# A third buffer for spectra and turned units, spectra asked for three slots ahead, and a later input turn, in a long-convolution and maxout kernel

## Chip, cores and metric

One Trainium2 chip, one of its cores. The metric is the device time of one execution in microseconds (us), the median of several runs. TensorE (PE) does the matrix products, VectorE (DVE), ScalarE (ACT) and GpSimd (POOL) the elementwise work; SyncE (SP) only issues DMAs here. Weight loads of TensorE stand in the profile as PEld. An engine's queue of instructions that it issues without computing has a "q" behind its name (SPq).

## What is computed

Four sequences (batches) of 12,544 positions with 128 channels go through a long convolution with a gate, and then through a feed-forward block with a maximum of three products:

```python
h_filt = (np.maximum(pos_emb @ w1, 0.0) @ w2) * window      # one filter per channel
u = x * v
y = irfft(rfft(u, n=2*S) * rfft(h_filt, n=2*S))[:, :S, :]   # along the positions
x = (x * y).reshape(B * S, D)
h = np.maximum(np.maximum(x @ w1, x @ w2), x @ w3)          # D = 128, DFF = 768
out = h @ w_out
```

All data are float32. The filter is so short in effect that the kernel needs only part of it; `lin` and the differences of weights let it do one of the three products of the feed-forward as a correction.

## The kernel before

**The convolution of one batch.** The Fourier transform is split into two stages of matrix products. The input of a batch comes in 32 units `u` (four channels each). A unit goes through these steps:

- `u_load` (L330): two DMAs on SP bring x and v of the unit into tiles `ut` of the pool `inq`, which has two buffers for each of the two (L856).
- `u_mul` (L342): DVE multiplies them in place.
- `u_planes` (L361): POOL clears the padding (L364) and splits the numbers into 16-bit halves (L365), into a tile `planes` of tag `x` (four buffers, `state["xb"]`).
- `u_dma` (L369): a transposing DMA on SP turns them, into `turned` of tag `xs` (five buffers, `state["xsb"]`).
- `u_join` (L375): ACT and DVE each put one half together again in a tile `uT` of the pool `utp` (two buffers; two units share a tile).
- `u_first` (L386): TensorE does the first stage, ACT or DVE copies the result into `spec`, which holds the whole batch.

Then follow 45 pairs `g` of frequencies. `w_load` (L393) brings the tables `wt` of the second stage (a = 0) and of the inverse stage (a = 1) from DRAM; they share tags and buffers with the `ut` tiles. `h_load` (L399) brings the filter's spectrum `ht` of the pair with two DMAs of SP; its tile has the tag `uT` of the pool `utp`, so spectra and turned units take turns in the same two buffers. `g_second` is the matrix product, `g_butterfly` (DVE) and `g_swap` (ACT) prepare the complex product, `g_re` (L430) and `g_im` (L433) multiply by the two halves of `ht` on DVE, `g_sum` (L436) adds on POOL, `g_unfold` (L442, tile `ab`) on DVE prepares the inverse, `g_third` is TensorE's inverse product, `g_pair` (L468) and `g_store` finish and send the result to DRAM (`zd`).

**The feed-forward.** Sixteen pairs of blocks of each batch, 12 steps (slots) each. `t_load` (L521) brings `zt` and the gate `xT` for a block with two and four DMAs on SP, `t_last` does the last stage of the inverse transform (TensorE, tile `yps`) and the gate (DVE, L558 and L560). In each slot `up` (L565) makes one hidden tile: two products `pa` and `pb` (TensorE), Relu of the first (ACT, L570), the maximum with the second (DVE, L573). POOL forms sums of hidden tiles (L589), and `products` (L608) makes the output products (L619), which are stored from ACT's queue. Hidden tiles named h11 have four buffers (`BUFS`, L584), as the others.

**What sets the order.** The schedule is written by hand: the program's order on each engine is the order in which the calls below are made. The prologue (up to L849) transforms the filter, runs the whole convolution of batch 0, and takes in the first six units of batch 1; in it `utp` holds turned units too. After that the main loop (L890) goes through the feed-forward of batch b and spreads the convolution of batch b + 1 over its 192 slots. `conv_steps` (L475) gives each step of the convolution a slot by a formula; steps of one slot run in the order in which `at` was called, those marked "late" last. For 32 units the distance of pairs `per_pair` is 165/64.2 = 2.57 slots and that of units 0.6 of it, 1.54; for batch 1, with 26 units left, 2.72 and 1.63. In a slot the loads for the feed-forward (`bring`) come first, in slots 0 and 1 of a pair of blocks, then `up`, the output products and sums, `t_last` in slots 5 and 8, and then the convolution's steps.

Every engine takes its instructions in the program's order. A DMA of SP that needs a buffer not yet free waits in SP's queue, and the DMAs behind it in the queue wait with it.

Of the kernel before, what the change touches and what calls it, by code (L numbers as in the profile page):

```python
# [70 lines left out]
def kernel(  # L71
# [147 lines left out]

    utp = ctx.enter_context(tc.tile_pool(name="utp", bufs=2))
    pro = ExitStack()
    pin = pro.enter_context(tc.tile_pool(name="pin", bufs=1))
    lwp = pro.enter_context(tc.tile_pool(name="lwp", bufs=3))
    eye = pin.tile([P, P], FP32, name="eye")
    w_sb[0] = pin.tile([D, DFF], FP32, name="w_sb0")
    inp = pro.enter_context(tc.tile_pool(name="inp", bufs=3))
    fin = ExitStack()
    inp0 = fin.enter_context(tc.tile_pool(name="inp0", bufs=3))  # L230
    sml = fin.enter_context(tc.tile_pool(name="sml", bufs=1))
# [243 lines left out]
    def conv_steps(b, done):  # L475


        out = []

        def at(slot, late, fn, *args):  # L480
            out.append((slot, late, len(out), fn, args))

        per_pair = 165 / (NK + 0.6 * (NU - done))
        for u in range(done, NU):
            s = (u - done) * 0.6 * per_pair + 12
            at(max(0, int(s) - 13), 0, u_load, b, u)
            at(int(s) - 8, 0, u_mul, u)
            at(int(s) - 7, 0, u_planes, u)  # L490
            at(int(s) - 6, 0, u_dma, u)
            at(int(s), 0, u_join, u)
            for h in range(2):
                at(int(s + 2 + 0.3 * per_pair * h), 1, u_first, u, h)
        s0 = int((NU - done) * 0.6 * per_pair) + 13
        for g in range(NK):
            s = s0 + int(g * per_pair)
            at(s - 5, 0, w_load, g, 0)
            at(s - 1, 0, h_load, g)
            at(s, 1, g_second, g)  # L500
            at(s + 1, 0, g_butterfly, g)
            at(s + 1, 0, w_load, g, 1)
            at(s + 2, 1, g_swap, g)
            at(s + 3, 0, g_re, g)
            at(s + 4, 0, g_im, g)
            at(s + 5, 0, g_sum, g, nc.gpsimd)
            at(s + 7, 0, g_unfold, g)
            at(s + 8, 1, g_third, b, g)
            at(s + 9, 0, g_pair, g)
            at(s + 10, 0, g_store, b, g)  # L510
        slots = {}
        for s, _, _, fn, args in sorted(out, key=lambda r: r[:3]):
            slots.setdefault(s, []).append((fn, args))
        return slots
# [50 lines left out]
    def up(i, f, tag, bufs):  # L565
        rhs = gs[i][:].rearrange("d p n -> d (p n)")
        h = hp.tile([P, N], FP32, tag=tag, name="hid", bufs=bufs)
        pa = hps.tile([P, 512], FP32, tag="hps", name="pa")
        halves_mm(pa[:, 0:N], w_sb[1][:, f * P:(f + 1) * P], rhs, True, True)
        nc.scalar.activation(h[:], pa[:, 0:N], Relu)  # L570
        pb = hps.tile([P, 512], FP32, tag="hps", name="pb")
        halves_mm(pb[:, 0:N], w_sb[2][:, f * P:(f + 1) * P], rhs, True, True)
        nc.vector.tensor_tensor(out=h[:], in0=h[:], in1=pb[:, 0:N], op=ALU.max)  # L573
        return h
# [6 lines left out]
    NC = NF // 2  # L581
    ORDER = (("h11", 0), ("h21", 0), ("h11", 1), ("h22", 0), ("h21", 1), ("h11", 2),
             ("h21", 2), ("h22", 1), ("h22", 2), ("h12", 0), ("h12", 1), ("h12", 2))
    BUFS = {"h11": 4, "h21": 4, "h22": 4, "h12": 4}  # L584
    NSTEP = len(ORDER)
    LAG = 9

# [131 lines left out]
    for f in range(0, FO, 4):  # L719
        quad([hs[:, f + i] for i in range(4)], f1h[:], specH[:, :, :, f:f + 4])  # L720
        u, k = divmod(f // 4, 4)
# [10 lines left out]
    for u in range(0, NU, 2):  # L732
        t = uts.pop(u)
        for v in range(2):
            if u + 4 < NU:
                u_mul(u + 4 + v)
            at = 4 * (u + v)
# [17 lines left out]
    cvp = pro.enter_context(tc.tile_pool(name="cvp0", bufs=3))  # L755
    cps = pro.enter_context(tc.tile_pool(name="cps0", bufs=3, space=PSUM))
    gps = pro.enter_context(tc.tile_pool(name="gps", bufs=2, space=PSUM))
    sps = pro.enter_context(tc.tile_pool(name="sps", bufs=1, space=PSUM))
    state = {"cv": (cvp, cps), "turn": cps, "xb": 2, "xsb": 2}
# [91 lines left out]

    hp = ctx.enter_context(tc.tile_pool(name="hp", bufs=3))
    inq = ctx.enter_context(tc.tile_pool(name="inq", bufs=5))
    f4p = hp.tile([N1, 2, NB // 2], FP32, name="f4p", bufs=1)
    nc.scalar.dma_start(f4p[:], f4p_d)
    inq = ctx.enter_context(tc.tile_pool(name="inq", bufs=2))  # L856
    cvp = ctx.enter_context(tc.tile_pool(name="cvp", bufs=3))
    cps = ctx.enter_context(tc.tile_pool(name="cps", bufs=3, space=PSUM))
    hps = ctx.enter_context(tc.tile_pool(name="hps", bufs=3, space=PSUM))
    ops = ctx.enter_context(tc.tile_pool(name="ops", bufs=1, space=PSUM))  # L860
    state = {"turn": cps, "cv": (cvp, cps), "xb": 4, "xsb": 5}
    banks = [ops.tile([P, 512], FP32, name=f"ops{i}") for i in range(2)]


# [15 lines left out]
    def bring(k, n):  # L880

        if k < len(pairs):
            t_load(pairs[k][0], pairs[k][1] + n)
# [6 lines left out]
    for k, (b, i) in enumerate(pairs):  # L890
        if i == 0:
            beside = {}
            if b + 1 < B:
                beside = conv_steps(b + 1, EARLY if b == 0 else 0)
# [6 lines left out]
        for j, (name, f) in enumerate(ORDER):  # L901
            n = int(name[1]) - 1
            if j in loads:
                bring(k + 1, loads.index(j))
            h[name, f] = up((b, i + n), f + (NC if name[2] == "2" else 0), name, BUFS[name])
            if j == 0:
# [56 lines left out]
```

## Time and profile before

| | |
|---|---|
| median of 5 runs | 2491.05 us (2487.71 to 2491.09) |
| the profiled execution, its own time | 2496.88 us |
| its span, first to last instruction | 2495.1 us |
| mean granted TensorE clock | 0.988 |
| busy: PE, PEld, DVE, ACT, POOL | 2382.2, 1668.5, 1508.6, 1007.4, 1150.2 us |
| DMA | 408.75 MB, mean 164 GB/s |

The stages in the span: the prologue takes about 325 us. Then the feed-forward of batch 0 with the convolution of batch 1 beside it (about 325 to 889 us), of batch 1 with that of batch 2 (889 to 1477), of batch 2 with that of batch 3 (1477 to 2068), and of batch 3 alone (2068 to 2495). In each of the three stages with a convolution the units come first (the "u stretch", some 50 slots) and then the pairs (the "g stretch", some 124 slots).

How to read it: a row of waits is "engine tile line <- what ended the wait: us in total, times, longest us". A row of the windows is the stretch, its length, busy time of PE, PEld, DVE, ACT and POOL with the number of instructions in brackets, then granted clock, DMA share and GB/s. A row of a timeline is the start and the duration in us, engine, line, operation, tiles written and read, and in brackets the idle time before it and what ended it. The page's table of DMA issues gives for each kind the median time from issue to landing: 4.1 us for `wt`, 4.6 for `ht`, 3.9 for `zt`, 4.2 for `turned`.

### The profile page before, as it was taken

Reading aid. Unit: us, or ns where it says so; the run is one execution under the profiler, and the core shown is the slowest. Engines: PE = TensorE matmul, PEld = TensorE weight load, DVE = VectorE, ACT = ScalarE, POOL = GpSimd, SP = SyncE. Lnnn points to the kernel's source line nnn. Section 1 sums busy time; section 2 is a strip of 40 time slices with the busy share of each in tenths; the row PEclk is TensorE's granted clock in tenths of the full one; section 3 lists DMA queues with packets and bytes.
Section 4 is the critical chain, followed back from the end, with each engine's and each line's share of the span. In section 5 each row is a group of like instructions: output and inputs, shape, how many; then the busy total and the mean of one; then the engine's idle time right before and its main releaser. Section 6 shows DMA issues by size and latency. Waiting matters only on the chain.

```text
span 2495.1 us, 71233 instructions
## 1 busy us (share of the span) xinstructions
PE 2382.2 (95%) x29025; PEld 1668.5 (67%) x29025; DVE 1508.6 (60%) x3044; ACT 1007.4 (40%) x1981; POOL 1150.2 (46%) x1204
## 2 busy tenths in 40 slices
PE   9999999999999999998899999999989899999998
PEld 9988867766666666766666666676666666666665
DVE  5588846576766645667676746567667663333333
ACT  2688824434434333444343423444434332222222
POOL 2022246444544555545454446544545454444444
PEclk9999999999999999999999999999999999999999
DMA  7789879677677578957777749967767753222220
GB/s 166 172 250 274 252 156 191 136 188 209 189 199 206 145 152 176 186 149 199 195 205 191 201 121 179 181 143 199 205 182 201 195 146 90 52 64 61 60 66 21
DMA packets 550737, 408.75 MB, mean 164 GB/s; under 512 B 396388, under 2 KB 442525, under 8 KB 550409
## 3 DMA queue, kind: packets, MB, share of 16 engines
q1 hardware_dynamic: 421760, 315.25, 52.3%
q10 hardware_dynamic: 123273, 74.33, 10.8%
q0 software_dynamic: 5376, 14.62, 2.1%
q8 instruction: 228, 3.74, 0.6%
q14 instruction: 100, 0.82, 0.1%
HBM read 295.76 MB, written 84.67 MB: 152 GB/s over the span
## 4 chain that ended last, share of the span: by engine, by line
PE 79%; DVE 9%; DMA 8%; issue 2%; SPq 1%; ACT 1%; DVEq 0%; ACTq 0%
PE ops L619 17%; PE pa L131 17%; PE pb L131 17%; PE ps L131 11%; PE ps L140 7%; PE yps L131 4%; PE sps L789 3%; DMA ht<-hd 3%; DVE ab L442 3%; DVE hid L573 1%; DMA zt<-zd 1%; DMA wt<-wt_const 1%; DVE zs L468 1%; DMA out_dram<-o 1%; PE gps L775 1%
## 5 line engine op out<-in xcount | busy, mean ns | idle before, releaser
L573 DVE TENSOR_TENSOR hid<-hid,pb 128x392 f32<-128x392 f32 x768 | 428.4, 558 | 471.2 <-PE pb L131 396.8
L570 ACT ACTIVATE hid<-pa 128x392 f32<-128x392 f32 x768 | 382.0, 497 | 700.5 <-PE pa L131 616.9
L131 PE MATMUL pa<-gt,w_sb 128*64 128x392 f32 x3072 | 645.3, 498 | 0.0
L131 PE MATMUL pb<-gt,w_sb 128*64 128x392 f32 x3072 | 641.6, 496 | 2.7 <-ACT hid L570 1.6
L131 PEld LDWEIGHTS pb<-gt,w_sb 128*64 128x64 f32 x3072 | 223.0, 138 | 292.9 <-issue 268.5
L589 POOL TENSOR_TENSOR s<-hid 128x392 f32<-128x392 f32 x192 | 208.4, 1086 | 333.7 <-DVE hid L573 327.7
L619 PE MATMUL ops<-hid,wo_sb 128*64 128x196 f32 x3072 | 332.7, 330 | 0.0
L436 POOL TENSOR_TENSOR xt<-xt,xs 128x512 f32<-128x512 f32 x135 | 172.2, 1276 | 313.0 <-DVE xs L433 258.8
L619 PEld LDWEIGHTS ops<-hid,wo_sb 128*64 128x64 f32 x3072 | 223.1, 138 | 139.0 <-issue 116.1
L589 POOL TENSOR_TENSOR s<-hid,s 128x392 f32<-128x392 f32 x192 | 201.7, 1052 | 218.8 <-DVE hid L573 217.0
L589 POOL TENSOR_TENSOR hid<-hid,s 128x392 f32<-128x392 f32 x192 | 215.2, 1126 | 96.7 <-DVE hid L573 70.7
L131 PE MATMUL ps<-ab,wt 128*64 128x128 f32 x2880 | 203.5, 278 | 50.3 <-DVE ab L442 45.1
L430 DVE TENSOR_TENSOR xt<-xt,ht 128x512 f32<-128x512 f32 x180 | 163.0, 905 | 144.8 <-DMA ht<-hd 130.4
L131 PE MATMUL ps<-spec,wt 128*64 128x128 f32 x2880 | 196.0, 280 | 34.7 <-DMA wt<-wt_const 16.8
L131 PEld LDWEIGHTS ps<-ab,wt 128*64 128x64 f32 x2880 | 164.0, 137 | 86.5 <-DVE ab L442 68.7
L131 PEld LDWEIGHTS pa<-gt,w_sb 128*64 128x64 f32 x3072 | 202.7, 139 | 19.3 <-issue 1.7
L589 POOL TENSOR_TENSOR hid<-hid 128x392 f32<-128x392 f32 x192 | 205.5, 1090 | 0.0
L442 DVE TENSOR_TENSOR ab<-xt 128x256 f32<-128x256 f32 x360 | 200.2, 596 | 1.6
L131 PEld LDWEIGHTS ps<-spec,wt 128*64 128x64 f32 x2880 | 169.3, 141 | 40.8 <-DVE zs L468 9.3
L140 PE MATMUL ps<-f,uT 98*64 98x90 f32 x4096 | 189.5, 243 | 5.7 <-ACT spec L144 4.8
L140 PEld LDWEIGHTS ps<-f,uT 98*64 98x64 f32 x4096 | 178.1, 138 | 15.0 <-ACT spec L144 7.6
L424 ACT ACTIVATE xs<-xt 64x512 f32<-64x512 f32 x180 | 113.1, 628 | 166.6 <-DVE xt L157 143.4
(103 smaller groups left out, 2845.2 us busy)
## 6 DMA issues: line engine op xcount, KB each, us to landing
wt<-wt_const SPq DMA_DIRECT2D x360, 256.0 KB, 4.1
ht<-hd SPq DMA_DIRECT2D x270, 256.0 KB, 4.6
zd<-zs ACTq DMA_DIRECT2D x180, 256.0 KB, 4.0
zt<-zd SPq DMA_DIRECT2D x192, 180.0 KB, 3.9
ut<-in_xr_dram SPq DMA_DIRECT2D x128, 196.0 KB, 3.6
ut<-in_vr_dram SPq DMA_DIRECT2D x128, 196.0 KB, 3.9
xT<-in_x_dram SPq DMA_DIRECT2D x512, 49.0 KB, 3.1
out_dram<-o ACTq DMA_DIRECT2D x512, 49.0 KB, 3.1
```

The costliest lines, as they stand in the source:

```text
L131: nc.tensor.matmul(out[64 * h:64 * h + 64], lhsT[:, 64 * h:64 * h + 64], rhs, start=start, stop=stop, skip_group_check=True)
L140: nc.tensor.matmul(ps[64 * c:64 * c + 64, 256 * i + r * N1:256 * i + (r + 1) * N1], a[:, r, :], table[:, c * N1:(c + 1) * N1], start=(i % ...
L424: nc.scalar.mul(xs[0:64], xt[64:128], -1.0)
L430: nc.vector.tensor_tensor(out=xt[:], in0=xt[:], in1=hts[g][:, 0], op=ALU.mult)
L436: eng.tensor_tensor(out=xts[g][:], in0=xts[g][:], in1=xss.pop(g)[:], op=ALU.add)
L442: nc.vector.tensor_tensor(out=ab[:, :, q, :], in0=y[:, :, 0, :], in1=y[:, :, 1, :], op=op)
L468: nc.vector.tensor_tensor(out=zs[:, a], in0=ps[:, 0:256], in1=z1[:], op=op)
L570: nc.scalar.activation(h[:], pa[:, 0:N], Relu)
L573: nc.vector.tensor_tensor(out=h[:], in0=h[:], in1=pb[:, 0:N], op=ALU.max)
L589: nc.gpsimd.tensor_tensor(out=out[:], in0=a[:], in1=b[:], op=op)
L619: nc.tensor.matmul(ps[64 * c:64 * c + 64, 0:H2], w, rhs[:, H2 * c:H2 * c + H2], start=start, stop=True, skip_group_check=True)
L789: nc.tensor.matmul(ps[64 * h:64 * h + 64, (2 * c + k) * 2 * D:(2 * c + k + 1) * 2 * D], G[:, k, c], w2x[:].rearrange("p s d -> p (s d)"), ...
```

## The change

Four things are edited together.

- The pool `utp` of the prologue (two buffers) moves into the prologue's own group of pools, which is closed at L849. For the main loop a new pool "utq" with three buffers takes the name `utp`, so `uT` and `ht` tiles there have three buffers.
- To make room, h11 has three buffers for four, and the tag `xs` of the main loop (`xs` and `turned`) four for five.
- `h_load` stands three slots ahead of `g_second` of its pair, where it stood one ahead.
- `u_mul`, `u_planes` and `u_dma` stand seven, six and five slots ahead of `u_join`, where they stood eight, seven and six ahead. `u_load` stays 13 slots ahead.

No operation is added or removed.

```diff
-    utp = ctx.enter_context(tc.tile_pool(name="utp", bufs=2))
     pro = ExitStack()
...
     inp = pro.enter_context(tc.tile_pool(name="inp", bufs=3))
+    utp = pro.enter_context(tc.tile_pool(name="utp", bufs=2))
...
             at(max(0, int(s) - 13), 0, u_load, b, u)
-            at(int(s) - 8, 0, u_mul, u)
-            at(int(s) - 7, 0, u_planes, u)
-            at(int(s) - 6, 0, u_dma, u)
+            at(int(s) - 7, 0, u_mul, u)
+            at(int(s) - 6, 0, u_planes, u)
+            at(int(s) - 5, 0, u_dma, u)
             at(int(s), 0, u_join, u)
...
             at(s - 5, 0, w_load, g, 0)
-            at(s - 1, 0, h_load, g)
+            at(s - 3, 0, h_load, g)
...
-    BUFS = {"h11": 4, "h21": 4, "h22": 4, "h12": 4}
+    BUFS = {"h11": 3, "h21": 4, "h22": 4, "h12": 4}
...
     inq = ctx.enter_context(tc.tile_pool(name="inq", bufs=5))
+    utp = ctx.enter_context(tc.tile_pool(name="utq", bufs=3))
...
-    state = {"turn": cps, "cv": (cvp, cps), "xb": 4, "xsb": 5}
+    state = {"turn": cps, "cv": (cvp, cps), "xb": 4, "xsb": 4}
```

## The prediction

> **What bounds the kernel now.** I read first the busy table, then the windows cut by stage, then each stage's waits, then the timelines around single waits.
>
> The windows (columns: stretch, its length, then busy time of PE, PE loads, DVE, ACT, POOL) show the spectrum-multiply stretches ("g") and the forward-transform stretches ("u") of the batches 1, 2, 3, and last the feed-forward alone:
>
> ```profile
> 348.00:473.00 125.00, 125.00 (x1704) 88.87 (x1702) 72.98 (x138) 51.93 (x100) 68.36 (x85) 1.00 0.87 175
> 473.00:875.00 402.00, 384.24 (x4314) 269.36 (x4312) 274.03 (x571) 161.66 (x336) 201.16 (x177) 0.99 0.69 185
> 915.00:1071.00 156.00, 151.62 (x2090) 106.85 (x2086) 90.55 (x171) 63.46 (x123) 88.40 (x109) 0.98 0.88 177
> 1071.00:1463.00 392.00, 360.54 (x4122) 247.64 (x4120) 274.21 (x557) 156.05 (x325) 192.16 (x168) 0.99 0.69 186
> ...
> 1657.00:2054.00 397.00, 361.46 (x4134) 249.19 (x4132) 275.94 (x558) 155.94 (x325) 192.02 (x169) 0.98 0.69 183
> 2094.00:2469.00 375.00, 375.00 (x3736) 227.64 (x3734) 134.32 (x276) 95.83 (x203) 174.00 (x174) 1.00 0.24 56
> ```
>
> TensorE is the bound everywhere: no idle in the last row, 4.4 us in batch 2's u stretch. Its idle time lies in the g stretches: 17.8, 31.5 and 35.5 us, together 84.8 us. That is all that a better feed can give back. The waits of one g stretch (1071 to 1463; PE, DVE, then SP's queue) say who is late:
>
> ```profile
> PE ps L131 <- DVE ab L442: 15.4, 21, 1.7
> PE ps L131 <- DMA wt<-wt_const: 6.3, 4, 2.7
> PE ps L131 <- DVE zs L468: 5.6, 4, 4.2
> ...
> DVE xt L430 <- DMA ht<-hd: 57.2, 23, 5.6
> ...
> SPq L396 <- PE ps L131: 108.4, 30, 8.8
> ```
>
> TensorE waits for VectorE, and VectorE waits 57.2 us for the spectrum ht. The same DVE row reads 12.7 us in batch 1's g stretch and 60.6 us in batch 3's. SP stands mostly at w_load, waiting for TensorE to give a wt buffer back.
>
> **What the Trainium skill says.** "Perfetto Trace Analysis", section "Per-engine timelines": VectorE, ScalarE and GpSimd are strictly first in, first out. The DVE timeline agrees: the next hid waits behind the multiply by ht, which had stood 3.88 us.
>
> ```profile
> 1201.66 0.55 DVE L573 TENSOR_TENSOR hid<-hid,pb 128x392 f32<-128x392 f32 x1
> 1206.09 0.69 DVE L430 TENSOR_TENSOR xt<-xt,ht 128x512 f32<-128x512 f32 x1 [3.88 <-DMA ht<-hd]
> 1206.70 0.56 DVE L573 TENSOR_TENSOR hid<-hid,pb 128x392 f32<-128x392 f32 x1
> ```
>
> "DMA: Bandwidth & Descriptors", section "Anatomy of one DMA — SWDGE (gpsimd) path": DMA engines never wait on semaphores, the issuing sequencer does. So a blocked load on SP holds every later one. The trace agrees: planes end at 991.4, the load that needs that buffer goes at 991.42, and the transpose queued behind it at 992.91. "Advanced Engine Details and Errata", section "X-Bar Transpose (TRN2)": transposing DMAs are as fast as plain ones. The issue table agrees: 4.2 us against 4.1 us for wt.
>
> **Part 1: ht three slots ahead, three buffers.** From conv_steps' formula pairs g stand 165/64.2 = 2.57 slots apart (batch 1: 165/60.6 = 2.72). SP's order around a pair was w0(g+2), w1(g), ht(g+1); it becomes w0(g+2), w1(g), ht(g+2). So each place in SP's order now carries the spectrum of one pair later. Its buffer wait is the same event too: with two buffers ht(g+1) waits for the multiply g-1, with three ht(g+2) does. SP is blocked no longer than before, the number of DMAs is unchanged, and each ht lands one pair, 2.57 x 3.16 = 8.1 us, earlier relative to its multiply (3.16 us a slot: 392 us over 124 slots). The longest ht wait in the trace is 5.9 us, so all 130.5 us of them (56 waits) should go. (The 14.0 us of L430 waiting for ACT's ht is the prologue's and stays.)
>
> What that is worth to TensorE I take from the batches against each other. The mean of batches 2 and 3 is 33.5 us idle at 58.9 us of ht waits; batch 1 has 17.8 at 12.7. The slope is 15.7/46.2 = 0.34, so 130.5 x 0.34 = 44 us. The remainder, about 13 us a batch, is VectorE late for other reasons and wt. Batches 2 and 3 have closer pairs than batch 1, so their remainder may be larger: I take **40 us gained**, bounds 20 (half of the link holds) and 60 (most of the 84.8 goes).
>
> **Part 2: u_mul, planes, transpose one slot later.** This is where time comes back. u_load's tiles have two buffers, so u_load(v) on SP waits for planes(v-2), and the transposes and next t_loads are queued behind it. In the u stretch SP therefore runs at the pace of planes, which follow u_mul by about 1 us. Shifting u_mul and planes by a slot (156/50 = 3.1 us) shifts everything behind u_load on SP by the same 3.1 us, while the joins and the t_last steps keep their slots.
>
> (a) *zt for the feed-forward.* In batch 2's u stretch the first t_last of each pair of blocks starts 3.9, 6.1, 6.5 and 4.9 us after its zt was issued (zt issue row against yps start in the timelines); batch 3: 4.4, 6.1, 6.0, 4.4. The landing takes 3.9 us; one such wait shows already:
>
> ```profile
> 930.50 1.14 PE L131 MATMUL yps<-f4p,zt 90*64 90x49 f32 x32 [0.62 <-DMA zt<-zd]
> ```
>
> With 3.1 us less (2.6 at the first, where slots are short) the new waits are 2.6+0.9+0.5+2.1 = 6.1 and 2.6+0.9+1.0+2.6 = 7.1, plus 1.1 for one second block that has 5.4 us. TensorE stands in order, so that is **14 us** in full. Batch 1 has 7 to 20 us: nothing.
>
> (b) *the joins.* From planes to join the last load ahead of a transpose left 4 slots (at times 5). By the same formula the change leaves 2 for 11 and 3 for most others of a batch's 32. Now a transpose is issued 5.9 to 6.1 us before its join in mid-stretch (985.87 to 991.99, 988.65 to 994.54) and needs 4.2: 1.8 spare. At 3 slots ACT waits 3.1-1.8 = 1.3 us, at 2 slots 4.4 us. What an ACT wait costs TensorE: the waits of 7.4 and 5.5 us in the trace stand beside 2.7 and 2.8 us of PE idle. So I price 1.3 at nothing (TensorE works ahead of ACT by more) and 4.4 at 0 to 1.9, taken as 0.4: 11 x 0.4 x 2 batches = 9 us. Behind the pair of t_loads (3.7 us of issue each) one more transpose a batch now stands behind both: about 7 us of wait, 2.7 each, **5 us** for two. The 9 overlaps with (a), since TensorE's own waits let ACT catch up: I count 8. Total of part 2: **27 us lost**, bounds 8 and 75 (next paragraph but one).
>
> **Parts with one answer.** BUFS of h11 3 for 4: all its products run in slot 9 of a pair of blocks, the next h11 begins in slot 12, and TensorE is in order: nothing. xsb 4 for 5: xs lives 3 slots at 2.57 a pair; the turned tiles need the join of four earlier, due 1 to 2 slots before and SP is later than its slot anyway: nothing, at worst inside (b). utp moved into the prologue and a new pool: same tiles, no operation added; bounded by +-3 us at the stage's start and for DMAs now ordered otherwise.
>
> **Sum.** The profiled execution took 2496.9 us (span 2495.1), 5.8 over the median of 2491.05. 2496.9 - 40 + 27 = 2484; against the median 2491 - 13 = **2478**.
>
> **Rivals.**
> *The u stretch becomes a closed loop (slower).* Where the margin is 2 slots there is a ring: join 15 on DVE 0.65, u_mul 20 behind it 0.7, planes 1.14, two loads' issue 0.9, transpose 4.2, join 17: 7.6 us plus five hand-overs, 0.1 each as an estimate (planes to load shows 0.03), about 8.1 per two units, against 2 x 1.54 x 3.1 = 9.6 us that TensorE takes for them. The t_loads add 7.4 us of SP per 12 slots, 1.9 a ring when not hidden: 10.0. Each us over 9.6 is TensorE idle. Some 10 rings a batch lie so, in two batches: at 2 us over, part 2 costs 27 + 40 = 67; at 1 us over, 47. It decides from about 0.7 us over (40 = 27 + 13). Likely value if it bites: **2491 - 40 + 67 = 2518**. For it: POOL already waits 33.0 us for turned in that stretch (18 times). Against: now VectorE is only 58% busy there, and mostly planes follow u_mul at once.
> *The u side costs little.* If the joins' waits are absorbed and TensorE's margins on zt hold: -44 + 8 = **2455**.
> *ht was a cover.* If wt and other VectorE lateness take the place of ht (slope 0.15 for 0.34), 20 gained against 27 lost: **2498**, or with a smaller loss no change, 2491.
>
> **Numbers.** Forecast (2468 to 2485) 0.36; little u cost (2440 to 2468) 0.20; cancelled, within 0.2% (2486 to 2496) 0.13; slower by ht as cover or the ring (2496 to 2535) 0.31. A measurement of this kernel tells about 0.2% from no change. The likeliest case's own range is 2468 to 2485; the range that should hold 8 in 10 reaches into both sides: 2448 to 2514.
>
> **What would show it.** ht waits of DVE gone and PE idle in the g stretches at 40 to 50 us instead of 85: part 1 right. PE waiting for zt in the u stretches of batches 2 and 3, about 14 us, and ACT's uT waiting for turned growing from 12 us a stretch to 40 or more: part 2 right. If zt waits stay at 1 us, SP did not shift. If u stretches of 156 us grow beyond 175, the ring holds. If g idle stays above 65 with ht waits gone, ht was a cover.

## The result, and the profile after

The change makes the kernel **slower**: 2508.2 us median of 20 runs (2489.6 to 2517.2) against 2492.2 for the kernel before (39 runs), a ratio of 1.0065, 95% interval 1.0054 to 1.0076. The profiled execution took 2509.16 us, its span 2507.0 us, against 2495.1 before: 11.9 us more.

The windows of the kernel after, cut at the same places in the program as those of before (length, busy time of PE, PE loads, DVE, ACT, POOL, granted clock, DMA share, GB/s):

```profile
348.00:475.00 127.00, 125.02 (x1698) 88.42 (x1696) 74.49 (x139) 51.91 (x99) 69.61 (x86) 1.00 0.94 180
475.00:876.00 401.00, 383.66 (x4324) 268.91 (x4322) 276.48 (x571) 161.86 (x336) 202.05 (x177) 0.99 0.69 184
916.00:1085.00 169.00, 154.85 (x2086) 108.25 (x2084) 91.69 (x172) 61.74 (x123) 92.31 (x111) 0.97 0.77 166
1085.00:1467.00 382.00, 357.52 (x4116) 255.27 (x4114) 277.03 (x556) 156.24 (x325) 195.34 (x168) 0.98 0.71 190
1507.00:1679.00 172.00, 157.91 (x2081) 112.89 (x2078) 90.39 (x171) 61.83 (x122) 90.21 (x109) 0.94 0.80 163
1679.00:2066.00 387.00, 362.55 (x4136) 256.19 (x4132) 277.91 (x558) 156.22 (x325) 196.11 (x169) 0.97 0.71 188
```

The same with the edges at the exact starts of the matmuls, as length (TensorE idle in it), in us:

| | u stretches, batches 1, 2, 3 | g stretches, batches 1, 2, 3 |
|---|---|---|
| before | 124.2 (0), 155.4 (4.4), 154.6 (4.5) | 402.7 (17.8), 391.9 (31.5), 396.6 (35.5) |
| after | 126.7 (2.0), 168.7 (14.2), 171.8 (14.1) | 400.8 (17.3), 382.8 (24.5), 386.5 (24.5) |
| difference of the sums | +33.0 (idle +21.4) | -21.1 (idle -18.5) |

So there is a gain in the g stretches and a larger loss in the u stretches, and 33.0 - 21.1 is the whole difference of the spans. The gain first. These are the waits of the g stretch of batch 2 (1085 to 1467) after the change, PE's and then the first of SP's queue:

```profile
PE ps L131 <- DMA wt<-wt_const: 12.4, 6, 5.0
PE ps L131 <- DVE ab L442: 11.1, 12, 1.7
...
SPq L396 <- PE ps L131: 81.7, 26, 6.3
```

VectorE's multiply no longer waits for the DMA of ht at all (130.4 us in the whole run before). But against the rows of this stretch before, which the prediction shows, TensorE's waits for `ab` only fell from 15.4 to 11.1 us, and those for the tables wt grew from 6.3 to 12.4. SP still stands 81.7 us at `w_load` (108.4 before).

The loss: waits of the kernel after in the u stretch of batch 2 (916 to 1085), all engines and SP's queue:

```profile
POOL planes L364 <- DMA turned<-planes: 53.3, 16, 11.1
ACT uT L380 <- DMA turned<-planes: 44.0, 15, 6.0
...
PE pb L131 <- ACT hid L570: 7.3, 7, 2.3
PE yps L131 <- DMA zt<-zd: 6.8, 3, 5.0
...
SPq L337 <- POOL planes L365: 42.1, 19, 3.0
```

The same rows of the kernel before (915 to 1071), where TensorE had no wait for ACT's Relus:

```profile
POOL planes L364 <- DMA turned<-planes: 33.0, 18, 8.1
ACT uT L380 <- DMA turned<-planes: 12.2, 4, 7.4
...
PE yps L131 <- DMA zt<-zd: 0.6, 1, 0.6
...
SPq L337 <- POOL planes L365: 18.7, 14, 3.2
```

ACT now stands 44 us at the joins; the Relus behind it come late, and TensorE waits for those (7.3 us) as much as for zt (6.8 us).

Why the turned units are late is seen in SP's queue. First the kernel before (start, duration, line, operation, tiles; "x2" means two such issues in a row, and the duration then runs from the start of the first to the end of the last, standing between them included):

```profile
985.87 1.23 SPq L371 DMA_TRANSPOSE turned<-planes  x1
987.60 0.37 SPq L337 DMA_DIRECT2D ut<-in_xr_dram  x1
988.02 0.54 SPq L337 DMA_DIRECT2D ut<-in_vr_dram  x1
988.65 1.46 SPq L371 DMA_TRANSPOSE turned<-planes  x1
991.42 0.37 SPq L337 DMA_DIRECT2D ut<-in_xr_dram  x1
991.84 0.98 SPq L337 DMA_DIRECT2D ut<-in_vr_dram  x1
992.91 1.23 SPq L371 DMA_TRANSPOSE turned<-planes  x1
```

and after:

```profile
986.76 0.37 SPq L337 DMA_DIRECT2D ut<-in_xr_dram  x1
987.18 0.79 SPq L337 DMA_DIRECT2D ut<-in_vr_dram  x1
988.06 2.75 SPq L371 DMA_TRANSPOSE turned<-planes  x2
993.87 0.37 SPq L337 DMA_DIRECT2D ut<-in_xr_dram  x1
994.34 0.46 SPq L337 DMA_DIRECT2D ut<-in_vr_dram  x1
996.12 0.37 SPq L337 DMA_DIRECT2D ut<-in_xr_dram  x1
996.54 1.01 SPq L337 DMA_DIRECT2D ut<-in_vr_dram  x1
997.64 2.60 SPq L371 DMA_TRANSPOSE turned<-planes  x2
```

Before, loads and transposes alternate. After, two units' loads stand together and two transposes follow. By conv_steps' formula (T a transpose, L a load, with the unit's number) the order around unit 17 was L17 T13 L18 T14 and became L17 L18 T13 T14. A load L(u) waits until the planes of unit u - 2 are made, so T13 now stands behind a load that waits for the planes of unit 16 instead of 15. By the formula 13 of the 32 transposes stand behind one more load than before, 9 of them behind that of the unit five later, as here, where none did.

### The profile page after: what moved, and what is told of

It reads as the page before. It is cut to its first block, busy times and chain, and to the rows that moved or that the text cites. A ratio compares the mean times of both kernels' runs of the same rounds, so it can differ in the third digit from the quotient of the medians.

```text
span 2507.0 us, 71264 instructions
## 1 busy us (share of the span) xinstructions
PE 2389.2 (95%) x29025; PEld 1692.9 (68%) x29025; DVE 1514.9 (60%) x3044; ACT 1004.6 (40%) x1981; POOL 1163.4 (46%) x1204
## 4 chain that ended last, share of the span: by engine, by line
PE 82%; DMA 8%; DVE 6%; issue 2%; SPq 1%; ACT 1%; ACTq 0%; POOL 0%; DVEq 0%; POOLq 0%
PE ops L619 18%; PE pb L131 17%; PE pa L131 17%; PE ps L131 12%; PE ps L140 7%; PE yps L131 5%; PE sps L789 3%; DMA wt<-wt_const 2%; DMA zt<-zd 2%; DMA turned<-planes 2%; DVE ab L442 2%; DMA out_dram<-o 1%; DVE hid L573 1%; DVE zs L468 1%; PE pm L304 1%
## 5 line engine op out<-in xcount | busy, mean ns | idle before, releaser
L131 PE MATMUL pb<-gt,w_sb 128*64 128x392 f32 x3072 | 644.7, 496 | 18.8 <-ACT hid L570 18.7
L589 POOL TENSOR_TENSOR s<-hid 128x392 f32<-128x392 f32 x192 | 214.0, 1115 | 304.4 <-DVE hid L573 278.0
L131 PE MATMUL ps<-spec,wt 128*64 128x128 f32 x2880 | 197.2, 280 | 29.2 <-DMA wt<-wt_const 21.1
L131 PEld LDWEIGHTS pa<-gt,w_sb 128*64 128x64 f32 x3072 | 206.0, 139 | 17.3 <-issue 1.5
L131 PEld LDWEIGHTS ps<-spec,wt 128*64 128x64 f32 x2880 | 170.8, 141 | 35.1 <-DVE ab L442 12.7
L430 DVE TENSOR_TENSOR xt<-xt,ht 128x512 f32<-128x512 f32 x180 | 171.2, 951 | 13.7 <-ACT ht L794 13.4
L619 PE MATMUL ops<-s,tw 128*64 128x196 f32 x1536 | 172.2, 330 | 0.0
```

Source lines behind the costliest of these rows:

```text
L131: nc.tensor.matmul(out[64 * h:64 * h + 64], lhsT[:, 64 * h:64 * h + 64], rhs, start=start, stop=stop, skip_group_check=True)
L430: nc.vector.tensor_tensor(out=xt[:], in0=xt[:], in1=hts[g][:, 0], op=ALU.mult)
L589: nc.gpsimd.tensor_tensor(out=out[:], in0=a[:], in1=b[:], op=op)
L619: nc.tensor.matmul(ps[64 * c:64 * c + 64, 0:H2], w, rhs[:, H2 * c:H2 * c + H2], start=start, stop=True, skip_group_check=True)
```

## Experiments

Every kernel was timed in five rounds beside the kernel before; ratios are to that, with 95% intervals.

### One part alone

**Spectra early, three buffers** (the change with the units' steps back in their old slots):

```diff
-            at(int(s) - 7, 0, u_mul, u)
-            at(int(s) - 6, 0, u_planes, u)
-            at(int(s) - 5, 0, u_dma, u)
+            at(int(s) - 8, 0, u_mul, u)
+            at(int(s) - 7, 0, u_planes, u)
+            at(int(s) - 6, 0, u_dma, u)
```

> The whole change, but u_mul, planes and the transposing DMA back at eight, seven and six slots ahead of the join. Theory A (the later input turn costs about 33 us in the u stretches, the earlier spectra gain about 21 us in the g stretches): about 2471 us (2465 to 2478), u stretches of batches 2 and 3 back at 155 us, PE idle in the three g stretches about 66 us, no ht wait. Theory B (the fourth turned buffer for five is what costs): stays above 2495. Theory C (the early spectra on SP are what delays the u stretch): stays above 2495 too.

Measured: 0.994 (0.9923 to 0.9957), 2484.9 us. No ht wait is left, TensorE idle in the g stretches 70.5 us. The part is a gain, of about 14 us, far from 40 and under the lower bound of 20.

**The units' steps later, nothing else** (kernel before):

```diff
-            at(int(s) - 8, 0, u_mul, u)
-            at(int(s) - 7, 0, u_planes, u)
-            at(int(s) - 6, 0, u_dma, u)
+            at(int(s) - 7, 0, u_mul, u)
+            at(int(s) - 6, 0, u_planes, u)
+            at(int(s) - 5, 0, u_dma, u)
```

> The kernel before, with only u_mul, planes and the transposing DMA one slot later (all buffers and the spectra as before). Theory A: about 2525 us (2515 to 2535), u stretches of batches 2 and 3 at 168 to 172 us, PE waits for zt of 5 to 7 us in each, g stretches unchanged. Theory B and theory C: 2492, nothing changes.

Measured: 1.0118 (1.0085 to 1.015), 2527.6 us. The u stretches take 126.6, 169.9 and 174.2 us; the g stretches hardly change (1195.0 us together, 1191.2 before). The parts add: 0.994 x 1.0118 = 1.0057, beside 1.0065 for the whole.

**Pools and buffer numbers alone** (the change, with the units' steps back as in the first experiment, and the spectrum too):

```diff
-            at(s - 3, 0, h_load, g)
+            at(s - 1, 0, h_load, g)
```

> The change's pools and buffer counts alone (third buffer for spectra and turned units, h11 three, xs and turned four); spectra and units at their old slots. Theory A: 2492 (2487 to 2497), u stretches as before, ht waits as before (about 130 us in all), since the slot and not the buffer binds. Theory B: 2505 or more with u stretches above 165.

Measured: 0.9995 (0.9981 to 1.001), idle in the g stretches 83.2 us, ht waits 129.6 us: nothing. A buffer without an earlier request gives nothing.

**Spectra early without the third buffer** (kernel before, one line):

```diff
-            at(s - 1, 0, h_load, g)
+            at(s - 3, 0, h_load, g)
```

> The kernel before with only the spectra asked for three slots ahead, in two buffers. The place of the spectrum in SP's order is one pair earlier, but its buffer comes free no earlier than before: SP then stands at it and holds the tables behind. If buffer and slot work only together: ht waits of DVE stay near 130 us in all, wt waits of PE grow, ratio 1.000 to 1.010. If the slot alone does it: ratio near 0.994 and no ht waits.

Measured: 1.0212 (1.0182 to 1.0242), 2550.9 us. The ht waits of VectorE go here as well (1.4 us are left), and yet 2.1% are lost, some 50 us; neither of the two expectations had both. Its waits over the whole run (PE's, then SP's queue at h_load):

```profile
PE ps L131 <- DMA wt<-wt_const: 68.4, 35, 6.2
...
SPq L403 <- DVE xs L433: 228.5, 59, 10.5
...
SPq L403 <- DVE hid L573: 121.3, 29, 10.9
```

A spectrum asked for before its buffer is free makes SP stand at h_load, and the tables behind it come late. With the tables where they are, slot and buffer work only together.

### The place in SP's queue

**Only the transpose later** (kernel before):

```diff
-            at(int(s) - 6, 0, u_dma, u)
+            at(int(s) - 5, 0, u_dma, u)
```

> The kernel before, with only the transposing DMA one slot later; multiply and planes at their old slots, so the loads on SP are released as before. Theory A1 (the cost comes through SP: planes later hold u_load, and with it zt and the transposes): 2492 to 2502, zt waits of PE at about 1 us a stretch, join waits a little up. Theory A2 (the shorter way from transpose to join is the cost by itself): about as much as the whole shift, 2515 or more.

Measured: 1.0093 (1.0068 to 1.0118), 2520.3 us. So most of the loss comes with this line alone, with the planes in their old slot; that the planes' shift is the cost, as I had put it, falls. The planes' shift may still add to the loss where the order is disturbed: TensorE waits 12.8 us for zt here and 22.9 us in the run before with both later. The intervals of the two ratios overlap, so how much it adds is not shown.

**The same, and the load one slot later too**, which restores the old order of loads and transposes on SP:

```diff
-            at(max(0, int(s) - 13), 0, u_load, b, u)
+            at(max(0, int(s) - 12), 0, u_load, b, u)
...
-            at(int(s) - 6, 0, u_dma, u)
+            at(int(s) - 5, 0, u_dma, u)
```

> The kernel with only the transposing DMA one slot later, and u_load one slot later too (12 slots ahead of the join for 13), so that on SP each transpose stands behind the same loads as in the kernel before. Theory Q (the place in SP's queue costs: one slot later puts half of the transposes behind one more u_load, and that waits for the planes of one more unit): the loss of 0.9% goes, ratio to before 0.997 to 1.003, join waits of ACT back at 12 us a u stretch. Theory S (five slots from transpose to join are too short by themselves): ratio stays at 1.007 or more.

Measured: 0.9978 (0.9964 to 0.9992), 2492.3 us. The u stretches of batches 2 and 3 in the windows, with the transpose alone later:

```profile
914.00:1079.00 165.00, 153.91 (x2086) 108.12 (x2084) 90.52 (x170) 62.24 (x123) 87.29 (x109) 0.97 0.85 167
1511.00:1676.00 165.00, 153.94 (x2088) 109.22 (x2086) 87.98 (x170) 62.16 (x123) 88.93 (x109) 0.97 0.87 167
```

and with the load later as well:

```profile
912.00:1062.00 150.00, 147.61 (x2070) 104.41 (x2068) 89.98 (x170) 63.90 (x122) 87.30 (x108) 1.00 0.96 184
1495.00:1647.00 152.00, 148.13 (x2084) 105.03 (x2082) 88.73 (x169) 63.97 (x123) 88.38 (x108) 1.00 0.95 180
```

ACT's waits at the joins in batch 2's stretch, with the transpose alone later:

```profile
ACT uT L380 <- DMA turned<-planes: 37.3, 13, 6.6
```

and with the load later as well:

```profile
ACT uT L380 <- DMA turned<-planes: 5.1, 3, 2.6
```

The transposes are the same in the same slots, and the only edit between the two is the load's slot, so what differs is what stands ahead of them in SP's queue. SP's standing at the unit loads for planes falls from 34.9 to 14.2 us in this stretch, and the stretch goes from 165 to 150 us.

**The whole change with the load at s-12:**

```diff
-            at(max(0, int(s) - 13), 0, u_load, b, u)
+            at(max(0, int(s) - 12), 0, u_load, b, u)
```

> The whole change with u_load at twelve slots for thirteen: units as in the change, but on SP in the same order against each other as in the kernel before. Theory Q: the order was the cost, ratio 0.992 to 0.997, u stretches of batches 2 and 3 at 152 to 157 us. If planes one slot later are a cost by themselves (SP then reaches the t_loads a slot later): zt waits of PE of 5 us and more in each stretch, u stretches above 160 us, ratio above 1.0.

Measured: 0.994 (0.9917 to 0.9964), 2487.0 us; u stretches 125.1, 155.7, 154.4. u_mul and u_planes are still a slot later here, zt's margins are back at 5.2, 6.2, 6.3 and 4.9 us, and TensorE waits 3.2 us for zt in the whole run. SP stands 17.9 us at the unit loads in batch 2's stretch (42.1 with the change). ACT stands 37.1 us at the joins there, little less than the 44.0 of the change, which by itself then costs little.

**The whole change with the load at s-10:**

```diff
-            at(max(0, int(s) - 13), 0, u_load, b, u)
+            at(max(0, int(s) - 10), 0, u_load, b, u)
```

> The whole change, with u_load ten slots ahead of the join for thirteen, close to the slot in which its buffer comes free, so that it doesn't hold SP's queue. Theory Q: the u stretches of batches 2 and 3 come back to 155 us or less, zt waits of PE under 1 us, ratio to before 0.990 to 0.995, like the spectra alone. Theory S: u stretches stay above 162 us, ratio above 1.002; loads that come later add waits of DVE for ut.

Measured: 0.9926 (0.9901 to 0.9951), 2482.6 us; u stretches 128.7, 153.1, 154.2. Again the loss is gone.

**Spectra early and the load at s-10** (on the first experiment's kernel, so that u_mul is at s-8):

```diff
-            at(max(0, int(s) - 13), 0, u_load, b, u)
+            at(max(0, int(s) - 10), 0, u_load, b, u)
```

> The spectra part alone (units at eight, seven and six slots) with u_load ten slots ahead for thirteen. Theory Q: at least as good as the spectra alone (0.994): 0.990 to 0.994, zt margins of 8 us and more in the u stretch; the gain is small, since the u stretches there hold only some 10 us of PE idle. If a load at ten slots lands too late for the multiply at eight: above 0.996, with DVE waits for ut above 30 us a stretch.

Measured: 1.0006 (0.9988 to 1.0025). This gives back the gain: with two slots between load and multiply VectorE waits 53.2 us for ut (18 times) in one u stretch, and the u stretches take 129.4, 166.4, 161.6 us. A load can also be too late.

**The last one with both tables later:**

```diff
-            at(s - 5, 0, w_load, g, 0)
+            at(s - 4, 0, w_load, g, 0)
...
-            at(s + 1, 0, w_load, g, 1)
+            at(s + 3, 0, w_load, g, 1)
```

> As the spectra part with u_load at ten slots, and w_load later: table 0 four slots ahead for five, table 1 three slots after for one, each close to when its buffer comes free. Theory W (what is left of PE idle in the g stretches comes from SP standing at w_load, so that tables and spectra come late): PE idle in the g stretches of batches 2 and 3 from 26 us to under 20, ratio 0.985 to 0.990. Theory V (what is left is VectorE's own order and load): PE idle there stays at 24 to 28, ratio as the run with u_load alone, or worse through wt waits.

Measured: 0.9984 (0.9963 to 1.0005). Idle in the g stretches 15.0, 26.2 and 28.4 us. As a test of the tables it is inconclusive: its u stretches are still spoilt, and table 0 was put later than its buffer comes free (by the formula at s - 2 x 2.57 = s - 5.1). It is no evidence against the tables, as the next group shows.

**Both good parts together** (on the first experiment's kernel, so that u_mul and u_planes are in their old slots):

```diff
-            at(max(0, int(s) - 13), 0, u_load, b, u)
+            at(max(0, int(s) - 12), 0, u_load, b, u)
...
-            at(int(s) - 6, 0, u_dma, u)
+            at(int(s) - 5, 0, u_dma, u)
```

> The spectra part (third buffer, three slots ahead) with units multiplied and split at their old slots, the transposing DMA one slot later and u_load at twelve slots for thirteen: the two good halves together. If u and g stretches don't touch each other: ratio to before 0.990 to 0.993 (0.994 of the spectra alone, 0.998 of the unit part), u stretches of batches 2 and 3 near 151 us, g stretches near 387 us. If the spectra take back what the units gain: 0.994 to 0.998.

Measured: 0.9906 (0.9883 to 0.993), 2476.4 us. It is the basis of the next group.

### Where the rest of the g stretches' idle time lies

Table 1 of pair g takes the buffer of pair g - 2, whose g_third runs at (s - 2 x 2.57) + 8 = s + 2.9. It is asked for at s+1, so by the formula SP stands there 1.9 slots, an estimated 6 us at 3.16 us a slot, and the next spectrum is behind it.

**Table 1 asked for at s+3** (on the basis):

```diff
-            at(s + 1, 0, w_load, g, 1)
+            at(s + 3, 0, w_load, g, 1)
```

> The spectra part with the unit part (0.991), and table 1 of a pair asked for three slots after g_second for one, nearer to when its buffer comes free. Theory W (SP stands at table 1's buffer and lets table 0 come late): wt waits of PE from 16 us to under 8 in batch 2's g stretch, PE idle there from 28 to 20, ratio 0.987. Theory V (the tables' two buffers, not their place in SP's order): wt waits stay above 12 us, ratio 0.990 to 0.993.

Measured: 0.9823 (0.9796 to 0.985), 2454.1 us. Idle in the g stretches 14.9, 18.3, 21.4.

**VectorE given a slot more ahead of the inverse product, table 1 left at s+1** (on the basis; 164 only so that the last step stays in the stage):

```diff
-        per_pair = 165 / (NK + 0.6 * (NU - done))
+        per_pair = 164 / (NK + 0.6 * (NU - done))
...
-            at(s + 8, 1, g_third, b, g)
-            at(s + 9, 0, g_pair, g)
-            at(s + 10, 0, g_store, b, g)
+            at(s + 9, 1, g_third, b, g)
+            at(s + 10, 0, g_pair, g)
+            at(s + 11, 0, g_store, b, g)
```

> As the run before, with g_third nine slots after g_second for eight, its pair and store one later, and the pairs 0.6% closer so that the last store keeps its slot. Theory V1 (what is left of PE idle in the g stretches is PE running ahead of VectorE and asking for ab one slot after it was made): PE waits for ab from 11 us a stretch to under 4, PE idle of the g stretches of batches 2 and 3 from 25 to under 17 us, ratio about 0.985. Theory V2 (VectorE is late as a whole): the waits only move to other rows (zs, wt, hid), idle stays at 24 to 28.

Measured: 1.0227 (1.02 to 1.0255), 2553.2 us. The waits of batch 2's g stretch (1099 to 1512; PE, then SP's queue):

```profile
PE ps L131 <- DMA wt<-wt_const: 44.4, 13, 6.5
...
SPq L396 <- PE ps L131: 150.5, 32, 8.6
```

No wait for `ab` is left, as wanted, but table 1's buffer now comes free a slot later, SP stands 150.5 us for the tables' buffers, and TensorE waits 44.4 us for tables.

**The control, 164 alone on the basis:**

```diff
-        per_pair = 165 / (NK + 0.6 * (NU - done))
+        per_pair = 164 / (NK + 0.6 * (NU - done))
```

> Control for the run with g_third later: the spectra part with the unit part, pairs and units 0.6% closer, and nothing else. If that spacing costs nothing: ratio 0.988 to 0.994, so that the loss of the run with g_third later is that step's own. If it does: above 1.0.

Measured: 0.9949 (0.9933 to 0.9965). The spacing costs something, some 0.4% against the basis, between what the two expectations named; it isn't what cost 77 us.

**Both: the inverse product later, and table 1 at s+4, where its buffer comes free** (on the kernel with the inverse product later):

```diff
-            at(s + 1, 0, w_load, g, 1)
+            at(s + 4, 0, w_load, g, 1)
```

> The run with g_third one slot later, and table 1 asked for four slots after g_second for one. Theory W: the wt waits of 44 us go to under 15, and as the ab waits are gone too, PE idle of batch 2's g stretch falls from 47 to under 20 us, ratio 0.985 or less. Theory V: wt waits stay above 25 us, ratio above 1.0.

Measured: **0.9613** (0.9585 to 0.9641), 2402.4 us, far below the 0.985 named. Neither step does this alone (0.9823 with the table later, to s+3, and 1.0227 with the inverse product later). The same waits of its batch 2 (1045 to 1404):

```profile
PE ps L131 <- DVE hid L573: 2.4, 1, 2.4
PE ps L131 <- DMA wt<-wt_const: 1.9, 2, 1.6
...
SPq L396 <- PE ps L131: 38.9, 22, 7.1
```

and the windows of its g stretches of batches 2 and 3:

```profile
1045.00:1404.00 359.00, 350.99 (x4134) 257.72 (x4132) 283.57 (x557) 156.60 (x325) 195.08 (x169) 1.00 0.75 203
1597.00:1957.00 360.00, 350.19 (x4134) 255.07 (x4132) 283.49 (x557) 156.74 (x326) 195.15 (x169) 1.00 0.76 202
```

**The same slots in the kernel before, with two buffers and the spectrum at s-1:**

```diff
-        per_pair = 165 / (NK + 0.6 * (NU - done))
+        per_pair = 164 / (NK + 0.6 * (NU - done))
...
-            at(max(0, int(s) - 13), 0, u_load, b, u)
+            at(max(0, int(s) - 12), 0, u_load, b, u)
...
-            at(int(s) - 6, 0, u_dma, u)
+            at(int(s) - 5, 0, u_dma, u)
...
-            at(s + 1, 0, w_load, g, 1)
+            at(s + 4, 0, w_load, g, 1)
...
-            at(s + 8, 1, g_third, b, g)
-            at(s + 9, 0, g_pair, g)
-            at(s + 10, 0, g_store, b, g)
+            at(s + 9, 1, g_third, b, g)
+            at(s + 10, 0, g_pair, g)
+            at(s + 11, 0, g_store, b, g)
```

> The kernel before (two buffers for spectra and units, spectra one slot ahead, h11 four, turned five) with the other steps of the best run: u_load at twelve, transposing DMA at five, table 1 at four slots after, g_third at nine. Theory X (the spectra were late only because SP stood at table 1): ratio 0.960 to 0.970 without the third buffer, ht waits of DVE under 30 us in all. Theory Y (the third buffer and the earlier slot are needed besides): ht waits stay above 80 us, ratio above 0.975.

Measured: **0.9619** (0.9593 to 0.9645), 2402.9 us, not to be told from the last. In the whole run VectorE waits for ht only this long:

```profile
DVE xt L430 <- DMA ht<-hd: 15.8, 16, 2.8
```

130.4 us became 15.8 without a third buffer and without an earlier slot for the request. By the formula table 1 of pair g, at s+1, stood ahead of the spectrum of pair g + 1; at s+4 it stands behind it. So with tables and inverse product in these slots the third buffer gives nothing that can be seen.

That table 1 alone made the spectra late is not shown: table and inverse product were moved together here, and SP stood at more than tables. The longest wait for ht in batch 2's g stretch before, 5.6 us, is that of pair 10 at 1165.34. This is SP's queue ahead of it:

```profile
1137.87 6.14 SPq L396 DMA_DIRECT2D wt<-wt_const  x2
...
1149.41 1.30 SPq L403 DMA_DIRECT2D ht<-hd  x2
1150.76 1.78 SPq L528 DMA_DIRECT2D zt<-zd  x2
1152.58 5.25 SPq L535 DMA_DIRECT2D xT<-in_x_dram  x4
1157.93 0.84 SPq L396 DMA_DIRECT2D wt<-wt_const  x2
1158.87 1.31 SPq L403 DMA_DIRECT2D ht<-hd  x2
```

In the first row SP stands 5.2 us at table 1 of pair 8. Then come the feed-forward's loads for two blocks; within the second (1152.58) SP stands 3.4 us until a store of the output has landed. Only then is the spectrum of pair 10 issued. Nine waits of over 3 us make up 40.8 of the 57.2 us in this stretch, and all nine are of spectra asked for in slots 0 to 3 of a pair of blocks, behind one or both of the feed-forward's loads in slots 0 and 1. How much of the late spectra is due to the tables, how much to these loads, and how much each of the last kernel's three moves (unit order, table 1, inverse product) gives without the others, stays open beyond the runs above.

## Why the prediction was wrong

The forecast was 2478 by -40 + 27; in the spans it was -21.1 + 33.0.

**Part 1, failed in its size, and this is the larger miss.** That all 130.5 us of ht waits go was right (130.4 to 0), and so was that SP is blocked no longer than before (108.4 to 81.7 us at the tables in batch 2). The step that failed is "The slope is 15.7/46.2 = 0.34". It measured 18.5 us of TensorE idle for 130.4, or 0.14, which is the rival "ht was a cover" (0.15) with its sign: idle time of 66.3 us, above the 65 named. Batch 1 differs from batches 2 and 3 in more than ht. Its pairs stand 2.72 slots apart instead of 2.57, which I had noted and for which I had taken only 4 us off. TensorE's waits for `ab` and the tables in its g stretch before (473 to 875) are:

```profile
PE ps L131 <- DVE ab L442: 14.0, 14, 2.5
...
PE ps L131 <- DMA wt<-wt_const: 1.0, 1, 1.0
```

The waits for `ab` are nearly those of batches 2 and 3 (15.4 and 15.1), at 12.7 us of ht waits against 57.2 and 60.6. The tables, 1.0 against 6.3 and 9.6, make 7.0 of the 15.7 us by which the stages differ, and the slope had put all of it down to ht. The rest is mostly short waits for other tiles of VectorE (`zs`, `hid`, `o`: none, against 8.2 and 7.6 us). So the slope of 0.34 was not that of ht alone. In the change the 20 us of the lower bound was nearly the value; alone the part gave about 14. What is left are `ab` (45.1 to 38.5 us in the whole run) and the tables (16.8 to 21.1). The two last experiments show what most of that hung on: with table 1 and the inverse product in other slots the g stretches have 20.6 and 21.4 us of idle time, with and without the third buffer.

**Part 2, its range right and its cause wrong.** 27 was named, with 8 to 75; the u stretches lost 33. As the larger term of it, (a), rested on another cause than the one found, this nearness is in part luck. Of the signs, the joins' waits were right (12.2 to 44.0 us a stretch; "40 or more"), and zt nearly: all waits of TensorE for zt in the run went from 3.6 to 14.3 us, 10.7 more for the 14 of (a). But (a) let the shift of planes carry the cost ("Shifting u_mul and planes by a slot ... shifts everything behind u_load on SP by the same 3.1 us"). With the planes at their old slot most of the loss is there (1.0093 of 1.0118, TensorE waiting 12.8 us for zt), and with the planes late and the order restored it is gone (0.994, the same as the spectra alone; 3.2 us for zt). So the cause is the transpose that drops behind one more blocked load, which (b) held for the smaller part ("leaves 2 for 11"), and SP's standing there makes zt late as well.

TensorE's idle time adds up: from the change to the change with its order restored it falls in the u stretches of batches 2 and 3 from 28.3 to 9.9 us, by 18.4; its waits for zt fall by 11.1 (14.3 to 3.2) and those for the Relus by 7.2 (18.7 to 11.5). The waits for the Relus, behind ACT's joins, were priced at 8 us in (b) and measured 17.1 more than before (1.6 to 18.7). ACT's own waits are a poor gauge of the loss: 37 us in batch 2's stretch stand beside a loss of 23 us in the kernel with only the transpose later, and beside next to nothing in the change with its order restored. The rest of the 33.0 us, 11.6, is TensorE busy longer (last section), for which no step of mine had a term. One term of (a) is also added wrongly: batch 3's first margin, 4.4 us less 2.6, leaves a wait of 2.1 and not 2.6 us, so the sum is 6.6 for 7.1; it changes nothing in the 14.

**The ring.** By its own sign, u stretches beyond 175 us, it is not shown: they became 169 and 172. In the window shown the transposes in pairs are 9.6 us apart, as long as TensorE was taken to need for two units. Over the stretch two units took 2 x 1.54 x 168.7/50 = 10.4 us. Whether the ring sets any part of this, or the feed-forward's loads between, was not separated.

**Parts with one answer.** Pools, `h11`, `xsb` at nothing: right (0.9995).

Why the signs came out as they did: the gain was taken 19 us too large, the loss 6 too small, and 25 us is more than the 13 that the sum had left. The measured time lies inside the wide range of 2448 to 2514, by way of a rival and not of the forecast.

## What to carry to other kernels

In a queue that issues in order, give a load the slot in which its buffer comes free: earlier it blocks what is behind it (1.0212 for the early spectrum with two buffers), too late and its reader waits (0.994 became 1.0006 with the unit load at s-10, two slots before its multiply). Where it has to be moved, list for each queue which blocked requests it passes. Before a buffer is added for data that comes late, look for what the issuing queue stands at ahead of it; here, with the table and the inverse product moved, the kernel was as fast without the third buffer as with it. A slope between stages may be used only when the stages differ in that one thing; comparing all rows of waits of the two stages shows whether they do.

## What was not expected of the hardware

Most stretches with more idle time also show a lower granted clock and more busy time for the same work. Of about 4130 matmul records, a g stretch of batch 2 shows 360.5 us busy at a granted clock of 0.99 before, and 351.0 at 1.00 in the best version; in the one with the inverse product later and the table early, 366.4 at 0.95 with 46.6 us idle. Likewise the u stretches: 151.6 busy at 0.98 before, 147.6 at 1.00 with transpose and load moved together, 157.9 at 0.94 after the change (batch 3). It isn't so for every pair of rows: batch 3's g stretch has 35.5 us idle at 0.98 and 361.5 us busy before, and 24.5 us idle at 0.97 and 362.6 us busy after. Of the best version's gain of 95.2 us in the three g stretches 64.2 are idle time, and the rest is TensorE busy for less time. Which causes which was not tested.

An issue of a transposing DMA holds SP's queue longer than a plain one: in the whole trace before the median of 90 is 1.31 us, against 0.39 and 0.51 for the two loads of a unit, though they land about equally fast (4.2 us, and 3.6 and 3.9 for these loads). A pair of transposes took 2.6 to 2.75 us in the timeline after.
